# Emitting a fused linear-attention and SwiGLU kernel from group 2 on by a list scheduler, with Strassen pairs spread over six groups

## The chip, the cores and the metric

The kernel runs on one core of a Trainium2 chip. The metric is device time in microseconds (us), as the median over several executions; the profiled execution has a span of its own, about 2 us shorter. A run's ratio is the mean time of its fast runs over the mean of the fast runs of the kernel before, taken on the same chip in the same rounds, so it is not quite the ratio of the two medians that are quoted.

The engines are PE (TensorE, matmuls; PEld is its weight load), DVE (VectorE), ACT (ScalarE), POOL (GpSimd) and SP (SyncE, which issues DMAs here).

## The reference, cut to what matters

```python
# q, k, v: (8 batches, 8 heads, 576 positions, 64); phi(x) = elu(x) + 1
kv  = einsum('bhsd,bhde->...', phi(k), v);  z = sum_s phi(k)
x   = (phi(q) @ kv) / (phi(q) . z + 1e-6)          # 4608 tokens x 512
h   = silu(x @ w_gate) * (x @ w_val)               # "first layer", 512 -> 1536
out = h @ w_out                                    # "second layer", 1536 -> 512
```

The 4608 tokens are cut into nine groups of 512. While PE works on the two layers of group g, the other engines prepare batch g+1 ("the chain": z broadcast, denominators, scaling of q, transposes by DMA) and batch g+2 (the features phi of k and q, then kv).

## The kernel before

The kernel is hand-scheduled: the order in which the program emits instructions is the order in which each engine runs its own. The lists of closures below fix that order. In groups 7 and 8, ten of the twelve feature blocks (128 features each) of the first layer are done as five Strassen-Winograd pairs: seven products of 256 columns instead of eight, for additions on VectorE and copies on ScalarE.

```python
    def load(src, dst, b):                       # two buffers for k16, q16, v16 (and kp, qp, vm)
        nc.gpsimd.dma_start(out=dst[b % 2][:, :, :], in_=heads(src, b))

    def plus_1(src, dst, b, lp):                 # phi: max(x, 0) + 1, then min with exp(x)
        nc.vector.tensor_scalar(out=dst[b % 2][...], in0=src[b % 2][...], scalar1=0.0, scalar2=1.0,
                                op0=ALU.max, op1=ALU.add)

    def tr(b, c):                                # chain, third c: DMA transpose of the scaled q
        nc.sync.dma_start_transpose(out=qT[b % 2][...], in_=qp[b % 2][...])

    def joint(b):                                # kv of batch b ("J"), then the diagonals of z
        for lp in range(2): mm1(b, lp)
        for lp in range(2): zdiag(b, lp)         # VectorE, PSUM -> zd
        r_copies(b)                              # ScalarE
    ...
    for g in range(1, NG):                       # cut
        for fb in range(FB if g in TS else 0, FB):
            l1(g, fb)                            # 8 matmuls of 512 columns, silu, product
            for f in sl[fb]: f()                 # zb (z broadcast, a matmul that reads zd) after fb 1 or 2,
                                                 # thirds of the chain spread over the blocks, h sums
        for (i, step) in enumerate(l2_steps(g)): # second layer as Strassen products 10 11 20 21 60 ...
            ...
            if i == 12: mm2(b1, ...)             # "M": x of the next group
            for f in pre[i]: f()                 # phi of batch g+2
            if i == 12 and b2 < B: joint(b2)     # "J" right after "M"
```

Of the kernel before, what the change touches and what calls it, by code (L numbers as in the profile page):

```python
# [17 lines left out]
def kernel(  # L18
# [52 lines left out]
    xT = [two([P, U * C], FP16, f"xT{i}") for i in range(4)]  # L71
# [12 lines left out]
    id16 = sb.tile([P, P], FP16, name="id16")  # L84
    idx = sb.tile([P, P], mybir.dt.int32, name="idx")
# [7 lines left out]

    def load(src, dst, b):
        nc.gpsimd.dma_start(out=dst[b % 2][:, :, :], in_=heads(src, b))  # L95
# [22 lines left out]
    def exp_(src, e, b, lp):  # L118
        s = slice(2 * lp, 2 * lp + 2)
        nc.scalar.activation(out=e[:, s, :], in_=src[b % 2][:, s, :], func=AF.Exp, bias=0.0, scale=1.0)  # L120

    def plus_1(src, dst, b, lp):
        nc.vector.tensor_scalar(
            out=dst[b % 2][:, :, P * lp:P * lp + P].rearrange("p j (s d) -> p s j d", d=D),
            in0=src[b % 2][:, 2 * lp:2 * lp + 2, :].rearrange("p s (j d) -> p s j d", d=D), scalar1=0.0, scalar2=1.0,
            op0=ALU.max, op1=ALU.add)

    def least(e, dst, b, lp):
        d = dst[b % 2][:, :, P * lp:P * lp + P].rearrange("p j (s d) -> p s j d", d=D)
        nc.vector.tensor_tensor(out=d, in0=d, in1=e.rearrange("p s (j d) -> p s j d", d=D), op=ALU.min)  # L130
# [18 lines left out]
    def vcast(b, lp):  # L149
        s = slice(2 * lp, 2 * lp + 2)  # L150
        nc.scalar.activation(out=vm[b % 2][:, :, s, 0:D].rearrange("p j l d -> p l j d"),  # L151
                             in_=v16[b % 2][:, s, :].rearrange("p l (j d) -> p l j d", d=D),
                             func=AF.Copy, bias=0.0, scale=1.0)
# [4 lines left out]
    def terms_k(b, lp):  # L158

        return (kp[1], kp[0]) if b == 0 else (kp[b % 2],)  # L160

    def mm1(b, lp):
        if lp == 0:
            kvb[b] = ((pV[2], pX[0]), (pX[2], pV[2]), (pX[0], pX[1]), (pV[0], pG[0]), (pX[2], pV[2]))[min(b, 4)]
        for j in range(J):
            for (t, term_) in enumerate(terms_k(b, lp)):
                for hh in range(2):
# [7 lines left out]
                    for e in range(2):  # L175
# [4 lines left out]
                            rhs=v16[b][rows, 2 * lp + e, D * j:D * j + D] if b < 2 else vm[b % 2][rows, j, 2 * lp + e, :],  # L180
                            start=(j == 0), stop=(j == J - 1))

    def zdiag(b, lp):
        for hh in range(2):
            nc.vector.tensor_scalar(out=zd[:, 2 * hh + lp, :], in0=id16[:, :],
                                    scalar1=kvb[b][hh][:, 256 * lp + D:256 * lp + D + 1],
                                    scalar2=1.0 / SC, op0=ALU.mult, op1=ALU.mult)

    def r_copies(b):
        W = D  # L190
        for hh in range(2):
            nc.scalar.activation(out=R[b % 2][:, hh:4:2, 0:W],
                                 in_=kvb[b][hh][:, :].rearrange("p (i c) -> p i c", i=2)[:, :, 0:W], func=AF.Copy,
                                 bias=0.0, scale=1.0)
# [16 lines left out]
    def zb_copy(b):  # L211
        for hh in range(2):
            rows = slice(C * hh, C * hh + C)
            nc.scalar.activation(out=zbc[rows, :], in_=zps[b][rows, 256 * hh:256 * hh + 256], func=AF.Copy,
                                 bias=0.0, scale=1.0)
# [5 lines left out]
    def s3_prod(b, c):  # L221
        j0, j1 = js_of(c)
        nc.vector.tensor_tensor(out=prod[:, 0:j1 - j0, :], in0=qp[b % 2][:, j0:j1, :],
                                in1=zbc[:, :].unsqueeze(1).to_broadcast([P, j1 - j0, HL * D]), op=ALU.mult)
# [13 lines left out]
    def s3_scale(b, c):  # L238
        j0, j1 = js_of(c)
        qv = qp[b % 2][:, j0:j1, :].rearrange("p j (l d) -> p (j l) d", d=D)  # L240
# [4 lines left out]
    def tr(b, c):  # L245
        j0, j1 = js_of(c)
        nc.sync.dma_start_transpose(out=qT[b % 2][:, j0:j1, :, :].rearrange("p j l t -> p (j l) t"),
                                    in_=qp[b % 2][:, j0:j1, :].rearrange("p j c -> p (j c)"))
# [5 lines left out]
    def corners(ps, lhs, b, j0, j1, lps=(0, 1)):  # L254

        for lp in lps:
            for hh in range(2):
                for e in range(2):
                    rows = slice(D * e, D * e + D)
                    nc.tensor.matmul(out=ps[2 * lp + e][C * hh:C * hh + C, :], lhsT=lhs(2 * lp + hh, e),  # L260
                                     rhs=qT[b % 2][rows, j0:j1, lp, C * hh:C * hh + C], start=True, stop=True)

    def mm2(g, ps, engs):
        us = units(g)
        c00 = 2 * C if g == 2 else 0
        for b in sorted(set(u[0] for u in us)):
            js = [j for (bb, j) in us if bb == b]
            c0 = C * us.index((b, js[0]))
            if b > 1:
                corners([x[:, c0:c0 + C * len(js)] for x in ps], kv(b), b, js[0], js[-1] + 1)  # L270
        for i in range(4):
            dst = xT[i][g % 2][:, c00:]
            if engs[i] == "A":
                nc.scalar.activation(out=dst, in_=ps[i][:, c00:], func=AF.Copy, bias=0.0, scale=1.0 / SC)
            else:
                nc.vector.tensor_scalar(out=dst, in0=ps[i][:, c00:], scalar1=1.0 / SC, scalar2=None, op0=ALU.mult)  # L276
# [25 lines left out]
    TS = (NG - 2, NG - 1)  # L302
    HN = U * C // 2
    sbanks = ((pG[0], pV[0]), (pG[1], pV[1]), (pX[2], pV[2]))

    def flat(t):
        return t[:, :, :].rearrange("p a b -> p (a b)")

    wr = rr[:, :, :].rearrange("p a b -> p (a b)").bitcast(FP16)
    wl_all = ((wr[:, 0:10 * P], wr[:, 10 * P:20 * P]), (wl2[:, 0, :], wl2[:, 1, :]), (flat(k16[0]), flat(q16[0])),  # L310
              (flat(v16[0]), flat(kp[0])))

    def wl(m, c, f0, f1):
        return wl_all[m][c][:, P * f0:P * f1]

    def wl_sum(m, c, f0, f1):
        (g1, g2, v1, v2) = [w[:, i, P * f0:P * f1] for (w, i) in ((wg, c), (wg, 2 + c), (wv, c), (wv, 2 + c))]
        (a, b, op) = ((v1, v2, ALU.add), (wl(0, c, f0, f1), g1, ALU.subtract), (g1, v1, ALU.subtract),
                      (g2, wl(1, c, f0, f1), ALU.subtract))[m]
        nc.vector.tensor_tensor(out=wl(m, c, f0, f1), in0=a, in1=b, op=op)  # L320

    def x_blk(g, kh, th, c):
        return xT[2 * kh + c][g % 2][:, HN * th:HN * th + HN]

    def x_sum(g, m, c):
        (a, b) = ((x_blk(g, 0, 1, c), x_blk(g, 0, 0, c)), (x_blk(g, 1, 1, c), xs[:, 0, c, :]),
                  (x_blk(g, 1, 1, c), x_blk(g, 0, 1, c)), (x_blk(g, 1, 0, c), xs[:, 1, c, :]))[m]
        nc.vector.tensor_tensor(out=xs[:, m, c, :], in0=a, in1=b, op=ALU.subtract)

    def sp_prd(g, p, n):  # L330
        dst = sbanks[p % 3][1 if n in (2, 3, 5) else 0]
        for e in range(2):
            for c in range(2):
                fs = slice(P * (2 * p + e), P * (2 * p + e) + P)
                lhs = {1: wg[:, c, fs], 2: wg[:, 2 + c, fs], 4: wv[:, 2 + c, fs]}
                lhs = lhs[n] if n in lhs else wl({3: 3, 5: 0, 6: 1, 7: 2}[n], c, 2 * p + e, 2 * p + e + 1)
                rhs = {1: x_blk(g, 0, 0, c), 2: x_blk(g, 1, 0, c), 3: x_blk(g, 1, 1, c), 4: xs[:, 3, c, :],
                       5: xs[:, 0, c, :], 6: xs[:, 1, c, :], 7: xs[:, 2, c, :]}[n]
                nc.tensor.matmul(out=dst[:, HN * e:HN * e + HN], lhsT=lhs, rhs=rhs,  # L339
                                 start=(n in (1, 2, 5) and e == 0 and c == 0), stop=(c == 1), skip_group_check=True)  # L340
# [4 lines left out]
    def f32(t, n):  # L345
        return flat(t).bitcast(FP32)[:, 0:n]

    def sp_bufs(p):
        i = p % 2
        s12 = f32((k16, v16)[i][1], 4 * HN).rearrange("p (i e t) -> p i e t", i=2, e=2)  # L350
        s5 = f32(q16[1], 4 * HN)[:, 2 * HN * i:2 * HN * i + 2 * HN].rearrange("p (e t) -> p e t", e=2)
        gg = f32((kp[1], ek)[i], 4 * HN).rearrange("p (h e t) -> p h e t", h=2, e=2)
        sl = vm[i][:, :, :, :].rearrange("p j l d -> p (j l d)")[:, 0:4 * HN].rearrange("p (h e t) -> p h e t", h=2, e=2)
        v22 = flat(prod)[:, 2 * HN * i:2 * HN * i + 2 * HN].rearrange("p (e t) -> p e t", e=2)
        return (s12[:, 0, :, :], s12[:, 1, :, :], s5), gg, sl, v22

    def sp_keep(p, i, from_z, scale=1.0):
        nc.scalar.activation(out=sp_bufs(p)[0][i], in_=halves(sbanks[p % 3][from_z]), func=AF.Copy, bias=0.0, scale=scale)

    def sp_gadd(p, th):  # L360
        (s, gg, _, _) = sp_bufs(p)
        nc.vector.tensor_tensor(out=gg[:, th, :, :], in0=halves(sbanks[p % 3][1]), in1=s[th], op=ALU.add)

    def sp_silu(p, th):
        (_, gg, sl, _) = sp_bufs(p)
        nc.scalar.activation(out=sl[:, th, :, :], in_=gg[:, th, :, :], func=AF.Silu, bias=0.0, scale=1.0)  # L366

    def sp_v22(p):
        (s, _, _, v22) = sp_bufs(p)
        nc.vector.scalar_tensor_tensor(out=v22, in0=halves(sbanks[p % 3][0]), scalar=SC, in1=s[2], op0=ALU.mult, op1=ALU.add)  # L370

    def sp_h21(g, p):
        nc.vector.scalar_tensor_tensor(out=hT[g % 2][:, 2 * p:2 * p + 2, 0:HN], in0=halves(sbanks[p % 3][0]), scalar=SC,
# [624 lines left out]
```

## Time and profile before

The time before was 305.57 us (three runs, 305.49 to 305.88). First, the page of the profile of the kernel before: its span, the busy time of each engine with its share and number of instructions, and the shares of the chain that ended last.

```profile
span 303.4 us, 6676 instructions
...
PE 295.6 (97%) x2596; PEld 181.0 (60%) x2596; DVE 247.6 (82%) x526; ACT 193.1 (64%) x313; POOL 49.2 (16%) x61
...
PE 89%; issue 4%; DMA 2%; ACT 1%; DVE 1%; POOL 0%; POOLq 0%; DVEq 0%; ACTq 0%
```

PE is the limit. Its busy time alone would not say so (matmuls overlap: the page gives one of 512 columns 379 ns, and the next one starts after 216), but the starts of the matmuls do. I took the distance of every two successive starts in the trace: 216 ns after a matmul of 512 columns and 109 ns after one of 256 is work; about 90 ns on top of that, at a change between matmuls on the full array and on quarters of it, is a mode change; what is above that is a wait. These sums are from 85 us (start of group 2) to the last matmul:

| kernel before | work | mode changes | waits |
|---|---|---|---|
| us | 211.4 | 1.0 | 0.9 |

Finally the DMA transposes of group 4 in the kernel before, from the view of one tile, qT, in a window from 150 to 182 us (first and last start, then the time from issue to landing):

```profile
L247 SPq DMA_TRANSPOSE qT<-qp x3: 1211/1211/1212, 158.6 to 168.9; - x3
...
DMA to landing us min/median/max: 2.7/2.7/2.7
```

They are issued between 158.6 and 168.9 us and land after 2.7 us. The kernel has two buffers for qp, so nothing of the next batch waits for them.

Of stretches (the view of windows), the busy time of VectorE was 28.4 of 31.5 us in each of groups 3 to 5.

### The profile page before, as it was taken

To read this page: it belongs to the slowest core of one execution; us is meant where nothing else is said; L and a number is where in the kernel's file an instruction comes from. 1 tells how busy PE (TensorE), PEld (TensorE's weight loads), DVE (VectorE), ACT (ScalarE), POOL (GpSimd) and SP (SyncE) were. 2 spreads that over 40 slices of the span, in tenths; PEclk is the share of its full clock that TensorE was granted. 3 is DMA by queue.
4 is the path that set the end of the run, shared out by engine and by line. 5 is a ranking of instruction groups with operands and counts; after the bars stand their busy time and mean duration, and the time that the engine had idled before them with its cause. 6 is when DMAs were issued, how large, how long until landed. Compare 5 with 4: busy or idle time off the path is not lost.

```text
span 303.4 us, 6676 instructions
## 1 busy us (share of the span) xinstructions
PE 295.6 (97%) x2596; PEld 181.0 (60%) x2596; DVE 247.6 (82%) x526; ACT 193.1 (64%) x313; POOL 49.2 (16%) x61
## 2 busy tenths in 40 slices
PE   7899999999999999999999999999999999999993
PEld 5644454444544485448644774477446888878882
DVE  4754649888859998998799889987999878968991
ACT  4864978858563698358846685568633478548931
POOL 8664256310010001000100000000000004001300
PEclk9999999999999999999999999999999999999998
DMA  8999999999979229911892132123312050033014
GB/s 214 193 196 201 206 208 220 199 212 191 133 147 154 51 31 201 190 34 29 173 197 56 28 81 62 34 46 71 71 26 54 22 119 0 2 74 67 2 37 104
DMA packets 41472, 32.88 MB, mean 108 GB/s; under 512 B 16400, under 2 KB 36816, under 8 KB 41440
## 3 DMA queue, kind: packets, MB, share of 16 engines
q0 software_dynamic: 20176, 18.35, 39.1%
q1 hardware_dynamic: 21104, 13.97, 20.1%
q8 instruction: 20, 0.33, 0.5%
q10 hardware_dynamic: 160, 0.13, 0.2%
q14 instruction: 12, 0.10, 0.1%
HBM read 37.75 MB, written 9.44 MB: 156 GB/s over the span
## 4 chain that ended last, share of the span: by engine, by line
PE 89%; issue 4%; DMA 2%; ACT 1%; DVE 1%; POOL 0%; POOLq 0%; DVEq 0%; ACTq 0%
PE pV L287 23%; PE pG L287 21%; PE pX L502 14%; PE pV L502 4%; PE pV L339 4%; PE pG L339 4%; PE pG L446 4%; PE pV L446 4%; PE pX L287 3%; DMA q<-in_q_dram 2%; PE pV L260 1%; PE pX L260 1%; PE pX L339 1%; PE pX L177 1%; PE pV L407 1%
## 5 line engine op out<-in xcount | busy, mean ns | idle before, releaser
L287 PE MATMUL pV<-xT,wv 128*128 128x512 f16 x324 | 83.5, 379 | 0.0
L287 PE MATMUL pG<-xT,wg 128*128 128x512 f16 x296 | 76.4, 379 | 0.0
L292 ACT ACTIVATE sil<-pG 128x512 f16<-128x512 f32 x74 | 43.5, 597 | 47.1 <-PE pG L287 32.2
L293 DVE SCALAR_TENSOR_TENSOR hT<-pV,sil 128x512 f16<-128x512 f32 x81 | 55.0, 686 | 15.0 <-PE pV L287 7.6
L287 PEld LDWEIGHTS <-wv 128*128 128x128 f16 x336 | 32.9, 98 | 39.7
L287 PEld LDWEIGHTS <-wg 128*128 128x128 f16 x336 | 32.3, 98 | 39.1 <-DVE xT L276 0.8
L502 PEld LDWEIGHTS <-hs 128*128 128x128 f16 x336 | 32.5, 98 | 4.7 <-DVE hs L476 0.4
L379 POOL TENSOR_TENSOR hT<-prod,vm 128x512 f16<-128x512 f16 x6 | 6.9, 1152 | 127.5 <-ACT vm L366 127.5
L502 PEld LDWEIGHTS <-hT 128*128 128x128 f16 x252 | 24.3, 98 | 4.1
L502 PE MATMUL pX<-ws,hs 128*128 128x256 f16 x210 | 25.7, 273 | 0.0
L507 ACT ACTIVATE part<-pX 128x256 f32<-128x256 f32 x35 | 12.8, 380 | 13.2 <-PE pX L502 13.2
L476 DVE TENSOR_TENSOR hs<-hT 128x512 f16<-128x512 f16 (+2 forms) x42 | 17.4, 418 | 0.2
L241 DVE TENSOR_TENSOR qp<-qp,rden 128x768 f16<-128x768 f16 x18 | 17.1, 948 | 0.0
L228 DVE TENSOR_REDUCE den<-prod 128x12 f32<-128x768 f16 x18 | 16.9, 942 | 0.0
L120 ACT ACTIVATE ek<-k 128x1152 f16<-128x1152 f16 x14 | 16.1, 1160 | 1.2 <-DMA k<-in_k_dram 1.1
L95 POOL DMA_DIRECT2D k<-in_k_dram x7 | 5.2, 745 | 64.1 <-ACT part L507 44.0
L502 PE MATMUL pX<-wo,hT 128*128 128x256 f16 x126 | 15.2, 273 | 0.0
L130 DVE TENSOR_TENSOR kp<-kp,ek 128x1152 f16<-128x1152 f16 x14 | 10.6, 758 | 5.4 <-ACT ek L120 5.0
L446 PEld LDWEIGHTS <-hT 128*128 128x128 f16 x96 | 8.7, 98 | 10.3 <-issue 0.8
L151 ACT ACTIVATE vm<-v 128x1152 f16<-128x1152 f16 x12 | 14.1, 1173 | 0.0
L120 ACT ACTIVATE eq<-q 128x1152 f16<-128x1152 f16 x12 | 13.3, 1169 | 0.0
L512 DVE SCALAR_TENSOR_TENSOR osb<-pX,part 128x256 f32<-128x256 f32 x28 | 11.0, 418 | 2.1 <-PE pX L502 1.9
(186 smaller groups left out, 513.7 us busy)
## 6 DMA issues: line engine op xcount, KB each, us to landing
out_dram<-osb SPq DMA_DIRECT2D x64, 128.0 KB, 3.0
k<-in_k_dram POOLq DMA_DIRECT2D x7, 576.0 KB, 8.8
q<-in_q_dram POOLq DMA_DIRECT2D x7, 576.0 KB, 11.4
v<-in_v_dram POOLq DMA_DIRECT2D x7, 576.0 KB, 13.5
wg<-in_moe_w_gate_dram POOLq DMA_DIRECT2D x5, 256.0 KB, 9.0
wv<-in_moe_w_val_dram POOLq DMA_DIRECT2D x5, 256.0 KB, 9.2
wo<-in_moe_w_out_dram POOLq DMA_DIRECT2D x2, 512.0 KB, 15.1
out_dram<-osb SPq DMA_DIRECT2D x13, 64.0 KB, 2.0
```

The source lines that it names most:

```text
L120: nc.scalar.activation(out=e[:, s, :], in_=src[b % 2][:, s, :], func=AF.Exp, bias=0.0, scale=1.0)
L151: nc.scalar.activation(out=vm[b % 2][:, :, s, 0:D].rearrange("p j l d -> p l j d"), in_=v16[b % 2][:, s, :].rearrange("p l (j d) -> p l j ...
L228: nc.vector.tensor_reduce(out=den[:, HL * j0:HL * j1], in_=prod[:, 0:j1 - j0, :].rearrange("p j (l d) -> p (j l) d", d=D), axis=AX.X, op=A ...
L241: nc.vector.tensor_tensor(out=qv, in0=qv, in1=rden[:, HL * j0:HL * j1].unsqueeze(2).to_broadcast([P, HL * (j1 - j0), D]), op=ALU.mult)
L287: nc.tensor.matmul(out=ps[:, :], lhsT=src[:, i, P * fb:P * fb + P], rhs=xT[i][g % 2][:, :], start=(i == 0), stop=(i == 3))
L292: nc.scalar.activation(out=s[:, :], in_=pg[:, :], func=AF.Silu, bias=0.0, scale=1.0)
L293: nc.vector.scalar_tensor_tensor(out=hT[g % 2][:, fb, :], in0=pv[:, :], scalar=SC, in1=s[:, :], op0=ALU.mult, op1=ALU.mult)
L339: nc.tensor.matmul(out=dst[:, HN * e:HN * e + HN], lhsT=lhs, rhs=rhs, start=(n in (1, 2, 5) and e == 0 and c == 0), stop=(c == 1), skip_gr ...
L446: nc.tensor.matmul(out=pso[(g, t)][:, :], lhsT=hT[g % 2][:, fb, P * t:P * t + P], rhs=wo[:, fb, :], start=(fb == 0), stop=(fb == FB - 1))
L476: (eng or nc.vector).tensor_tensor(out=o, in0=a, in1=b, op=op)
L502: nc.tensor.matmul(out=(z if n in (2, 3, 5) else x)[:, 0:HD], lhsT=left(f), rhs=right(f), start=(f == 0 and n in (1, 2, 5)), stop=(f == HF ...
L507: nc.scalar.activation(out=part[:, 2 * i + tt, :], in_=(x if from_x else z)[:, 0:HD], func=AF.Copy, bias=0.0, scale=1.0 / SC)
```

## The change

The change has three intents. From group 2 on, a list scheduler orders the instructions instead of the hand-made lists: every operation is declared with its engine, a modelled duration, and the names it reads and writes; a simulation with modelled durations and lags then picks the order for ScalarE and VectorE (PE, GpSimd and SyncE keep the program's order). Strassen pairs go from ten to 24: two in each of groups 3 to 5, six in each of 6 to 8. And product 1 of a pair is copied by ScalarE into another PSUM bank (PSUM is the memory that matmuls write to, here the tiles pG, pV and pX), on which product 2 accumulates, which takes one addition per pair off VectorE. To hold the extra weight sums, the even buffers of k16, q16, v16, kp and vm are given up from batch 3 on: one function, `ix`, decides the buffer. The diff has over 900 lines; this is its core:

```diff
+    def ix(b):
+        return b % 2 if b < 3 else 1
+
     def load(src, dst, b):
-        nc.gpsimd.dma_start(out=dst[b % 2][:, :, :], in_=heads(src, b))
+        nc.gpsimd.dma_start(out=dst[ix(b)][:, :, :], in_=heads(src, b))
 ...
     def plus_1(src, dst, b, lp):
-            out=dst[b % 2][:, :, P * lp:P * lp + P]...,
-            in0=src[b % 2][:, 2 * lp:2 * lp + 2, :]...,
+            out=dst[ix(b)][:, :, P * lp:P * lp + P]...,
+            in0=src[ix(b)][:, 2 * lp:2 * lp + 2, :]...,
 ...
     def tr(b, c):
-                                    in_=qp[b % 2][:, j0:j1, :]...)
+                                    in_=qp[ix(b)][:, j0:j1, :]...)
 ...
+    wl_all = [sum((thirds(t) for t in ts), []) for ts in (
+        (k16[0][:, :, :], q16[0][:, :, :], v16[0][:, :, :]), (kp[0][:, :, :], wl2[:, :, :], vm[0][:, :, :, :]))]
 ...
+    LAG = dict(PE=0.2, ACT=0.18, DVE=0.18, POOL=0.3, SP=2.7, LD=9.0)
+    ops = []
+    def op(eng, t, f, r=(), w=()):
+        ops.append((eng, t, f, tuple(r), tuple(w)))
+    def arrange():            # cut: dependencies from the names, then at each step the ready
+        ...                   # operation that can start first; within 0.2 us, the most urgent
+    NP = {2: 0, 3: 2, 4: 2, 5: 2, 6: 6, 7: 6, 8: 6}
 ...
+        if n == 1:
+            op("ACT", 0.52, lambda: keep_1(bx, halves(by)), [nm(bx)], [nm(by)])      # the seed
 ...
+    ZB = {g: 2 for g in range(NG)}                    # z broadcast after 2 chunks (0.86 us) of a group
+    XE = {g: "AVAA" for g in range(NG)}               # engines of the four x copies
+    ORDER = {g: "10 11 20 21 60 61 50 51 70 71 30 M 31 40 J 41" for g in (2, 3, 4)}
+    ORDER[5] = "10 11 20 21 60 61 50 51 70 71 M 30 31 | 40 41 J"
 ...
+    program()
+    for i in arrange():
+        ops[i][2]()
```

## The prediction

> **What bounds it now.** TensorE. In the page it is busy 97% and PE work is 89% of the chain that ended last. In the timeline from group 2 on, matmul starts are 216 ns (512 columns) or 109 ns (256 columns) apart almost without a break: start-to-start distances beyond those two sum to about 2.0 us between 85 and 298 us, mostly the ~93 ns at each change between full and quarter-array matmuls (M and J steps). So a better order has almost no PE wait to remove. VectorE is second: 28.5 of 31.5 us busy per group in groups 3 to 5 (windows).
>
> **Removed from PE.** Two plain feature blocks are 16 x 216 = 3.456 us; one Strassen pair is 28 x 109 = 3.056 us; a pair saves 0.40 us. Pairs go from 10 (five in groups 7 and 8) to 24 (two in 3-5, six in 6-8): 14 more, so 5.6 us: 0.8 in each of groups 3-5, 2.4 in group 6, 0.4 in 7 and 8.
>
> **Added to PE.** M and J are no longer adjacent (groups 2-5) and M is split in 6-7: two more array mode changes each, 6 x 0.19 = 1.1 us. Waits of 0.07-0.10 us at group boundaries may go (-0.3). Floor: 305.6 - 5.6 + 1.1 - 0.3 = about 300.8 us.
>
> **Other engines.** Durations in the profile overlap: back to back the 686 ns PSUM product on VectorE recurs every 601 ns, reduce 860, scale 866, prod 411, least 676, 128x512 fp16 sum 335, ScalarE activation 493. (The Trainium skill, "Perfetto Trace Analysis", Per-instruction lifecycle, says the window holds the write acknowledgement; this trace agrees, 686 against 601.) With these a pair costs VectorE 3 x 601 + 335 = 2.1 us against 1.2 for the plain blocks (the PSUM seed has already removed one 0.6 us add). ScalarE: 5 x 0.5 against 2 x 0.5. Estimated VectorE issue time per group after: group 2 31.9 us (eight weight sums of 0.47 added), 3 and 4 30.4, 5 29.9, group 6 about 28, against PE 31.6, 30.9, 30.9, 28.4. Before: about 27.3 of 31.5. So VectorE has no slack in groups 2-6, and its in-order queue will at times hold what PE needs. I estimate 1-2 us of new PE waits there, and about 0.3 us in each of groups 6-8 after the sixth pair, where no plain blocks are left to cover its latency.
>
> The seed costs no PE time: ScalarE copies product 1 into another bank and product 2 adds there. The Trainium skill, "PSUM — Partial Sum Buffer", The four PSUM rules, says ScalarE writes leave the accumulate bits alone; no run here shows it yet.
>
> **Prediction.** 300.8 + about 1.6 = 302.4 us; 8 in 10 between 300.7 and 304.5. Faster by over 2%: 0.05; within 2%: 0.92; slower: 0.03.
>
> **What would show it.** Windows: group 6 shorter by about 2 us, 7-8 hardly, groups 3-5 by only 0.2-0.6 us each, group 2 longer by 0-0.5. VectorE busy over 95% in groups 2-5. Waits: new PE (weight load) waits on VectorE hT, hs, xs or on xT. Up to group 2 and after the last matmul: unchanged. If groups 3-5 each gain 0.6 us, VectorE was not limiting.
>
> **What would make it wrong.** The static order's modelled lags (loads 9 us, transposes 2.7 us) may differ from the chip: ScalarE could block on a value cast for some us. Or the order hides VectorE and the floor is reached.

## More of the kernel before

The batches of runs were taken on several chips, and the kernel before took 305.4 to 305.9 us in them; a small difference between runs of different batches is therefore read from the ratios.

The timeline of VectorE in the kernel before, at the end of group 4 (start us, duration us, engine, line, operation, output<-inputs, count, and in brackets the idle time before and what ended it):

```profile
178.00 1.29 DVE L276 TENSOR_SCALAR xT<-pG 128x512 f16<-128x512 f32 x2 [0.75 <-PE pG L260]
179.21 0.25 DVE L185 TENSOR_SCALAR zd<-id,pX 128x128 f16<-128x128 f16 x1
...
179.70 0.25 DVE L185 TENSOR_SCALAR zd<-id,pV 128x128 f16<-128x128 f16 x1
179.87 0.45 DVE L123 TENSOR_SCALAR qp<-q 128x1152 f16<-128x1152 f16 x1
```

The four diagonals of z (`zd`) come first and the next batch's query features (`qp<-q`) behind them. The timeline of PE at the same place:

```profile
181.95 1.03 PE L287 MATMUL pV<-xT,wv 128*128 128x512 f16 x4
182.81 0.38 PE L208 MATMUL pX<-zd,ones 128*128 128x512 f16 x1
183.03 1.03 PE L287 MATMUL pG<-xT,wg 128*128 128x512 f16 x4
```

The z broadcast (`pX<-zd,ones`) starts 3.46 us into group 5 (179.35 us) and waits for nothing.

## The result, and the profile after

The change took 310.69 us (four runs, 309.70 to 311.52) against 305.60 us for the kernel before in the same rounds: ratio 1.0164, 95% interval 1.013 to 1.0198. It is 1.6% slower where I had predicted 1% faster, and outside the range that I gave.

The page after, the same lines:

```profile
span 309.4 us, 7044 instructions
...
PE 294.9 (95%) x2764; PEld 197.7 (64%) x2764; DVE 262.6 (85%) x561; ACT 217.1 (70%) x361; POOL 42.4 (14%) x55
...
PE 47%; issue 38%; DVE 6%; DMA 5%; ACT 1%; POOL 1%; POOLq 0%; DVEq 0%
```

| from 85 us to the last matmul, us | work | mode changes | waits |
|---|---|---|---|
| before | 211.4 | 1.0 | 0.9 |
| after | 206.6 | 1.9 | 10.2 |

The share of "issue" in the chain, 4% before and 38% now, is time for which the view finds no releaser; it is a sign that PE no longer runs through, and the sums of the distances say how much. So the saving is there: 4.8 us of work by these sums, and up to 5.7 us in the variants below, for the 5.6 that I had predicted. The mode changes cost 0.9 us (predicted 1.1). But PE waits 9.3 us longer. By groups the waits are 0.7 (group 2), 0.3, 2.1, 4.7, 0.9, 0.9 and 0.6 us (group 8): the two largest lie at the starts of groups 4 and 5. Apart from the half clock described below, no other single wait of PE is longer than 0.7 us. The view of waits of the change (who waited for whom: us in total, times, longest) names both:

```profile
PE pX L214 <- DVE zd L193: 3.6, 2, 2.3
DVE qp L128 <- DMA qT<-qp: 3.4, 2, 2.0
```

The timeline of VectorE in the change, at the end of group 4 and the start of group 5:

```profile
180.91 0.42 DVE L336 TENSOR_TENSOR xs<-xt 128x512 f16<-128x512 f16 x1
183.29 0.46 DVE L128 TENSOR_SCALAR qp<-q 128x1152 f16<-128x1152 f16 x1 [1.97 <-DMA qT<-qp]
183.67 0.26 DVE L193 TENSOR_SCALAR zd<-id,pX 128x128 f16<-128x128 f16 x1
...
185.04 0.26 DVE L193 TENSOR_SCALAR zd<-id,pV 128x128 f16<-128x128 f16 x1 [0.34 <-ACT R L198]
```

VectorE stands still for 1.97 us. The query features of batch 6 (`qp<-q`) wait for the third DMA transpose of batch 5, which still reads the same buffer. The diagonals of z stand behind them in the queue, though their own input has been there since the J matmuls, about 181 us. The timeline of PE at the same place:

```profile
182.00 1.03 PE L934 MATMUL pG<-xt,wg 128*128 128x512 f16 x4
185.35 0.59 PE L214 MATMUL pX<-zd,ones 128*128 128x512 f16 x1 [2.32 <-DVE zd L193]
185.73 1.06 PE L934 MATMUL pV<-xt,wv 128*128 128x512 f16 x2
```

The z broadcast waits 2.32 us for the diagonals, and the matmuls behind it wait as long. In the kernel before, VectorE had the diagonals first, and the broadcast stood 2.6 us later in the group. The qT tile of the change, from 164 to 186 us:

```profile
L251 SPq DMA_TRANSPOSE qT<-qp x2: 1310/1334/1359, 176.7 to 178.2; - x2
...
  DVE qp L128: 2.0, 1
...
DMA to landing us min/median/max: 5.0/5.4/5.9
```

The third transpose of group 4 is issued 29.3 us after the start of the group (178.2 less 148.9 us), before it was 21.1 us (168.9 less 147.8), because VectorE comes to the third part of the chain late; the last two transposes are issued 1.5 us apart, and they take 5.9 and 5.0 us to land, not 2.7. The k load of batch 7 is in flight: it was issued at 175.39 us and landed after 6.37 us. The Trainium skill, "Trainium Kernel Development and Optimization", Key Constraints, says that DMAs issued from SyncE, ScalarE and GpSimd run on the same 16 DMA engines and interleave. This trace agrees: from group 2 on, the transposes that overlap a load take 3.1 to 5.9 us, the others 2.7 to 2.8, with one of 3.6. A short overlap need not show: in the kernel before, two transposes that overlapped the end of a v load for 1.6 to 1.7 us still took 2.7 us.

That VectorE cannot pass a waiting instruction is what the Trainium skill says too ("PSUM — Partial Sum Buffer", Engine vs sequencer instructions: the queues of ScalarE, VectorE and GpSimd are strict first in, first out), and the trace agrees with 1.97 us in which ready work stood behind.

Windows of the change at this wait (length; busy us and count of PE, PEld, VectorE, ScalarE and GpSimd; then the granted clock of PE, DMA share and GB/s):

```profile
183.00:184.00 1.00, 0.03 (x1) 0.00 (x0) 0.63 (x2) 0.04 (x1) 0.00 (x0) 1.00 1.09 391
184.00:184.90 0.90, 0.00 (x0) 0.00 (x0) 0.43 (x2) 0.41 (x2) 0.00 (x0) 1.00 0.93 209
184.90:185.70 0.80, 0.35 (x1) 0.10 (x1) 0.66 (x3) 0.80 (x3) 0.00 (x0) 0.63 0.17 59
185.70:188.30 2.60, 2.60 (x10) 1.22 (x9) 2.40 (x5) 1.39 (x4) 0.43 (x1) 0.50 0.46 102
```

The wait has an echo: PE's clock is halved from 185.11 to 188.52 us (3.41 us by the trace's clock record), which costs about 1.5 us more by the distances of the starts. The Trainium skill, "TensorE: Matmul & The Clock Gate", What's actually happening, describes a half-rate state set by a free-running window of 3413 ns, and the length agrees. It also fits the spread of the four runs: 309.70 and 310.25 us came with a mean granted clock of 0.997, 311.12 and 311.52 us with 0.992 and 0.994. That the latter two had one more window at half clock is my reading; only the profiled one (311.12 us) has a trace.

### The profile page after: what moved, and what is told of

It is laid out like the page before. It is cut to its first block, busy times and chain, and to the rows that moved or that the text cites. A ratio compares the mean times of both kernels' runs of the same rounds, so it can differ in the third digit from the quotient of the medians.

```text
span 309.4 us, 7044 instructions
## 1 busy us (share of the span) xinstructions
PE 294.9 (95%) x2764; PEld 197.7 (64%) x2764; DVE 262.6 (85%) x561; ACT 217.1 (70%) x361; POOL 42.4 (14%) x55
## 4 chain that ended last, share of the span: by engine, by line
PE 47%; issue 38%; DVE 6%; DMA 5%; ACT 1%; POOL 1%; POOLq 0%; DVEq 0%
PE pV L934 7%; PE pG L934 6%; PE pV L293 6%; PE pX L440 5%; PE pG L293 4%; PE pX L293 4%; PE pG L379 4%; PE pV L379 3%; DMA qT<-qp 3%; PE pX L347 2%; DMA q<-in_q_dram 2%; PE pX L264 1%; PE pV L440 1%; DVE zd L193 1%; DVE qp L135 1%
## 5 line engine op out<-in xcount | busy, mean ns | idle before, releaser
L934 PE MATMUL pV<-xt,wv 128*128 128x512 f16 x144 | 39.8, 386 | 0.0
L934 PE MATMUL pG<-xt,wg 128*128 128x512 f16 x144 | 38.4, 379 | 0.0
L364 ACT ACTIVATE sil<-pG 128x512 f16<-128x512 f32 x36 | 21.4, 593 | 22.6 <-PE pG L934 21.4
L440 PEld LDWEIGHTS <-hs 128*128 128x128 f16 x336 | 32.4, 98 | 5.2 <-issue 1.0
L440 PEld LDWEIGHTS <-hT 128*128 128x128 f16 x252 | 24.1, 98 | 4.7 <-DVE hs L409 0.4
L370 DVE SCALAR_TENSOR_TENSOR hT<-pV,sil 128x512 f16<-128x512 f32 x36 | 24.6, 682 | 0.8 <-PE pV L934 0.7
L934 PEld LDWEIGHTS <-wv 128*128 128x128 f16 x144 | 14.2, 99 | 15.1 <-issue 2.9
L347 PEld LDWEIGHTS <-wg 128*128 128x128 f16 x192 | 18.9, 99 | 5.6 <-issue 1.0
L293 PE MATMUL pV<-xt,wv 128*128 128x512 f16 x84 | 21.9, 379 | 0.0
L299 DVE SCALAR_TENSOR_TENSOR hT<-pV,sil 128x512 f16<-128x512 f32 x21 | 14.2, 689 | 9.0 <-ACT sil L298 4.9
L934 PEld LDWEIGHTS <-wg 128*128 128x128 f16 x144 | 14.1, 98 | 11.9
L364 ACT ACTIVATE ek<-eq 128x512 f16<-128x512 f32 x24 | 15.0, 624 | 7.2 <-DVE eq L963 7.1
L347 PE MATMUL pV<-xt,wg 128*128 128x256 f16 x120 | 17.0, 273 | 0.0
L440 PE MATMUL pX<-wo,hT 128*128 128x256 f16 x126 | 16.9, 273 | 0.0
L449 ACT ACTIVATE part<-pX 128x256 f32<-128x256 f32 x35 | 12.4, 389 | 6.1 <-PE pX L440 6.0
L293 PEld LDWEIGHTS <-wv 128*128 128x128 f16 x96 | 9.4, 98 | 11.3
```

Of the source, the lines that this page charges most:

```text
L293: nc.tensor.matmul(out=ps[:, :], lhsT=src[:, i, P * fb:P * fb + P], rhs=xT[i][g % 2][:, :], start=(i == 0), stop=(i == 3))
L299: nc.vector.scalar_tensor_tensor(out=hT[g % 2][:, fb, :], in0=pv[:, :], scalar=SC, in1=s[:, :], op0=ALU.mult, op1=ALU.mult)
L347: nc.tensor.matmul(out=dst[:, HN * e:HN * e + HN], lhsT=lhs, rhs=rhs, start=(n in (1, 5) and e == 0 and c == 0), stop=(c == 1), skip_group ...
L364: nc.scalar.activation(out=dst, in_=src, func=AF.Silu, bias=0.0, scale=1.0)
L370: nc.vector.scalar_tensor_tensor(out=hT[g % 2][:, fb, :], in0=pv[:, :], scalar=SC, in1=s[:, :], op0=ALU.mult, op1=ALU.mult)
L440: nc.tensor.matmul(out=(z if n in (2, 3, 5) else x)[:, 0:HD], lhsT=left(f), rhs=right(f), start=(i == 0 and fs[0] == 0 and (n in (1, 5) or ...
```

## The experiments

Eighteen kernels were run in five batches, all correct. The theories:

- Theory 1: the qp buffer shared by successive batches makes VectorE wait for a transpose, and all that stands behind waits with it.
- Theory 2: VectorE is full, as the prediction had it; the waits are lack of throughput.
- Theory 3: the z broadcast merely stands too early in PE's order.
- Theory 4: the scheduler's modelled lags (transposes 2.7 us, loads 9.0 us) are too short, so the static order puts instructions ahead of others that turn out to be ready sooner.
- Theory 5: any reshuffle gives another time; what a constant does is luck.
- Theory 6: the transposes land late because they overlap the k load.

In the texts, "the third run" is e3_np0 and "the fourth run" e4_splag. All results in one table. "Waits" are PE's, with matmuls at half clock, as defined above; the ratio is to the kernel before in the same rounds.

| kernel | time, us | ratio | work | mode changes | waits |
|---|---|---|---|---|---|
| the change | 310.69 | 1.0164 | 206.6 | 1.9 | 10.2 |
| e1_qp2 | 307.43 | 1.0057 | 206.1 | 1.9 | 6.8 |
| e2_zb8 | 308.43 | 1.009 | 205.9 | 1.8 | 8.2 |
| e3_np0 | 311.19 | 1.0182 | 208.6 | 1.9 | 7.8 |
| e4_splag | 305.12 | 0.9983 | 206.6 | 1.9 | 4.2 |
| e5_lags | 307.02 | 1.0042 | 206.3 | 1.8 | 6.5 |
| e6_np0_lags | 305.87 | 1.0003 | 208.6 | 1.9 | 2.7 |
| e7_qp2_lags | 305.51 | 0.9994 | 205.7 | 1.9 | 5.3 |
| e8_splag4 | 305.88 | 1.0012 | 206.2 | 1.9 | 5.5 |
| e9_relief | 310.38 | 1.017 | 206.0 | 1.9 | 10.0 |
| e10_qp2_relief | 308.10 | 1.0089 | 205.7 | 1.9 | 7.9 |
| e11_qp2_rel_mj | 308.04 | 1.0085 | 206.6 | 1.4 | 8.0 |
| e12_relief_only | 319.30 | 1.0453 | 206.4 | 1.8 | 18.1 |
| e13_qvk | 307.81 | 1.0073 | 206.5 | 1.9 | 6.6 |
| e14_qp2_xact | 304.39 | 0.9959 | 206.0 | 1.9 | 4.3 |
| e15_np1 | 305.46 | 0.9993 | 207.4 | 1.4 | 4.5 |
| e16_np0_mj | 305.95 | 1.0011 | 208.3 | 1.4 | 3.7 |
| e17_m1 | 304.66 | 0.9964 | 206.1 | 1.6 | 4.4 |
| e18_m1_mj | 305.37 | 0.9986 | 206.6 | 1.1 | 5.4 |

### e1_qp2: two buffers for the query features, same order

```diff
+    def iq(dst, b):
+        return b % 2 if dst is qp else ix(b)
-            out=dst[ix(b)][:, :, P * lp:P * lp + P]...      # plus_1 and least
+            out=dst[iq(dst, b)][:, :, P * lp:P * lp + P]...
-    ... qp[ix(b)] ...                                        # product, scale, transpose of the chain
+    ... qp[b % 2] ...
```

> The only edit: the query features of batches 3 on get two buffers again (batch parity), as in the kernel before. The order on every engine is unchanged, checked instruction by instruction. Theory 1 (shared buffer): the longest PE waits (1.4 us in group 4, 2.5 us plus 1.4 us of half clock in group 5) come from VectorE standing still 1.4 and 2.0 us at the head of its queue, where the next batch's query features wait for the third transpose of the batch before, out of the same buffer. Then those VectorE waits vanish and the time falls by 4 to 5.5 us, to 305 to 307. Rival, theory 2 (VectorE is simply full): the wait at the z broadcast matmul stays or moves, and the time stays above 309.

It took 307.43 us (306.90 to 307.77). The even qp buffer had been free all along: the weight sums do not use it. The order of instructions on every engine is the same, and so is VectorE's work, so only the wait is taken away. The timeline of VectorE in e1_qp2 at the place shown above:

```profile
179.67 0.42 DVE L339 TENSOR_TENSOR xs<-xt 128x512 f16<-128x512 f16 x1
180.00 0.46 DVE L131 TENSOR_SCALAR qp<-q 128x1152 f16<-128x1152 f16 x1
180.37 0.26 DVE L196 TENSOR_SCALAR zd<-id,pX 128x128 f16<-128x128 f16 x1
```

VectorE no longer stands still, the wait at the z broadcast falls to 0.4 us in group 5 and to nothing over 0.1 us in group 4, and the clock is not halved there. About 3.3 us of the 5.1 us loss are gone. Theory 1 holds for that part; it falls 0.4 us short of the range that I wrote down, for 6.8 us of waits remain, at more places than before (the largest 1.1 us).

### e2_zb8: the z broadcast later on PE

```diff
-    ZB = {g: 2 for g in range(NG)}
+    ZB = {g: 8 for g in range(NG)}
```

> The z broadcast matmul stands after 8 chunks of the first layer instead of 2 (about 5 us later on PE); the list scheduler then orders VectorE and ScalarE anew. Theory 3 (the wait is only placed too early on PE): PE no longer waits there, 305 to 306.5. Theory 1: the VectorE waits of 1.4 and 2.0 us stay, PE is shielded from most of them: 306 to 308. Theory 2: PE waits turn up at other matmuls, time 309 to 312.

It took 308.43 us, just above what theory 1 expected and below theory 2. No wait at the broadcast is left, but 8.2 us of waits are, spread over the pairs and the starts of products, and VectorE still stands 1.8 us at the transpose. Placing was a part, not the cause. ScalarE and VectorE were reordered with it, so this run is a weaker test than the first.

### e3_np0 and e6_np0_lags: no pairs in groups 3 to 5, without and with longer lags

```diff
-    NP = {2: 0, 3: 2, 4: 2, 5: 2, 6: 6, 7: 6, 8: 6}
+    NP = {2: 0, 3: 0, 4: 0, 5: 0, 6: 6, 7: 6, 8: 6}                               # both
-    LAG = dict(PE=0.2, ACT=0.18, DVE=0.18, POOL=0.3, SP=2.7, LD=9.0)
+    LAG = dict(PE=0.2, ACT=0.18, DVE=0.18, POOL=0.3, SP=5.0, LD=13.0)             # e6_np0_lags only
```

> No Strassen pairs in groups 3 to 5, six in 6 to 8 as in the change: 6 pairs less, so PE has 2.4 us more and VectorE about 2.2 us less in each of the three groups. Theories 1 and 2 both: VectorE finishes the chain earlier, the third transposes are issued earlier, the waits in groups 4 and 5 shrink below 0.5 us; net 306 to 307.5. If the pairs were not the cause of the lateness but the scheduler's order were, the waits stay and the time rises to about 313.

It took 311.19 us, against 306 to 307.5 expected: a miss, and the one that taught most. VectorE has about 2 us less to do in each of the three groups (two pairs at 2.1 against 1.2 us, by the estimate of the prediction), yet PE waits 7.8 us. The view of waits of e3_np0 shows where:

```profile
ACT vm L156 <- DMA v<-in_v_dram: 7.0, 4, 2.9
```

With time to spare, the scheduler puts the cast of v on ScalarE as soon as its model has the load landed. The trace has v landing 10.9 to 12.4 us after issue; the model has 9.75. ScalarE stands 7.0 us in all, the activations behind it wait, and PE waits for their products. VectorE also stands 1.5 us at a transpose. That is theory 4 at a second place.

> No pairs in groups 3 to 5 as in the third run, with transposes at 5.0 and loads at 13.0 us in the model. In the third run ScalarE stood 7.0 us on value loads and VectorE 1.5 us on a transpose. Theory 4: both waits vanish, PE waits fall from 7.8 us to below 3.5: 306 to 308 (PE work is 2.4 us more than with the pairs). If VectorE work rules, it should even beat the run with pairs. If it stays near 311, theory 4 falls.

With both lags longer, the same kernel took 305.87 us; the 7.0 us and the 1.5 us are gone and PE's waits fall from 7.8 to 2.7 us. Two constants of the model are worth 5.3 us here, with the same PE order. Without the pairs in groups 3 to 5 and with the model's old lags the kernel is as slow as the change. A loss of that size thus needs no pairs there; but it sits mostly at another wait (ScalarE at the casts), so this does not show that the waits of the change itself would have come without them.

### e4_splag, e8_splag4, e5_lags: the lags alone

```diff
-    LAG = dict(PE=0.2, ACT=0.18, DVE=0.18, POOL=0.3, SP=2.7, LD=9.0)
+    LAG = dict(PE=0.2, ACT=0.18, DVE=0.18, POOL=0.3, SP=5.0, LD=9.0)     # e4_splag
+    LAG = dict(PE=0.2, ACT=0.18, DVE=0.18, POOL=0.3, SP=4.0, LD=9.0)     # e8_splag4
+    LAG = dict(PE=0.2, ACT=0.18, DVE=0.18, POOL=0.3, SP=5.0, LD=13.0)    # e5_lags
```

> One constant of the scheduler's model: a transpose is taken to land 5.0 us after issue instead of 2.7 (measured here 2.8 to 5.9). Same PE order. Theory 1: the scheduler then puts the diagonals of z ahead of the query features that wait, or issues the transposes sooner, and the PE waits in groups 4 and 5 shrink: 306 to 309. Theory 2: 309.5 to 312, as before.

> Transpose lag 4.0 us, loads 9.0 as in the change: between the change (2.7) and the fourth run (5.0). Theory 4: the measured landings of the third transposes are 3.9 and 5.0 us, so 4.0 helps in part, 305 to 308, monotonic in the lag. Theory 5: no order, may be worse than 310.

> The change with both lags of the scheduler's model set to what the traces show: transposes 5.0 us (was 2.7) and loads 13.0 us (was 9.0; value loads took 8 to 12.4). PE order unchanged. Theory 4 (the static order is wrong because the modelled lags are too short, and in-order queues then stand still): at least as good as with the transpose lag alone, 304 to 305.3. Rival, theory 5 (any reshuffle gives another time, the lag was luck): anywhere from 304 to 311.

They took 305.12, 305.88 and 307.02 us. One constant, the transpose lag, takes the change from 310.69 to 305.12 us. The timeline of VectorE in e4_splag at the end of group 4:

```profile
179.74 0.42 DVE L336 TENSOR_TENSOR xs<-xt 128x512 f16<-128x512 f16 x1
180.08 0.25 DVE L193 TENSOR_SCALAR zd<-id,pX 128x128 f16<-128x128 f16 x1
...
184.19 0.82 DVE L128 TENSOR_SCALAR kp<-k 128x1152 f16<-128x1152 f16 x2
184.93 0.46 DVE L128 TENSOR_SCALAR qp<-q 128x1152 f16<-128x1152 f16 x1
```

The diagonals come first now, and the query features start 4.9 us after them; the transpose, issued at 179.85 us, has landed by then (after 3.28 us). The times fall with the lag: 310.7, 305.9 and 305.1 us for 2.7, 4.0 and 5.0. But with the longer load lag as well, the kernel is 1.9 us slower than without it: a miss. The 6.5 us of waits in e5_lags have a new largest one of 1.1 us before kv of batch 7. So theory 4 explains the large waits: none of the three kernels has a wait of VectorE at a transpose left. Theory 5 is right about the rest: the order alone moved the time by 1.9 us between e4_splag and e5_lags. What about the order makes that difference was not found, and how much of the 5.6 us that e4_splag returns is such luck is not known.

### e7_qp2_lags: lags and buffer together

```diff
+    (as e1_qp2, and the scheduler's names for qp by batch parity, as e5_lags for the lags)
+    def rqp(b, c=(0, 1, 2), lps=(0, 1)):
+        return [f"qp{b % 2}.{lp}.{k}" for lp in lps for k in c]
```

> Both lags as before, and two buffers for the query features, of which the scheduler now knows (names by batch parity). Theory 1 with 4: one more constraint gone, 303 to 305. If VectorE is simply full, no gain over the run with lags alone: within 0.5 us of it.

It took 305.51 us, 1.5 us less than e5_lags, but half a microsecond above the range. The second buffer is worth less once the model's lags are longer; e5_lags has no wait of VectorE at a transpose left for it to remove. The 1.5 us are within what a new order can do by itself.

### e12_relief_only, e9_relief, e10_qp2_relief, e11_qp2_rel_mj: VectorE relieved

```diff
-    XE = {g: "AVAA" for g in range(NG)}
+    XE = {g: "AAAA" for g in range(NG)}
-                pair_prd(g, p, PSEQ[0][k], (pX[1], pX[0])[p % 2], pX[2], pV[1], "DVE")
+                pair_prd(g, p, PSEQ[0][k], (pX[1], pX[0])[p % 2], pX[2], pV[1], "POOL")
     # e12_relief_only: nothing else;  e9_relief: SP=5.0
     # e10_qp2_relief: as e7_qp2_lags; e11_qp2_rel_mj: as e10, and ORDER "... 30 31 40 M J 41" in groups 2 to 4
```

> The change with VectorE relieved of about 1.3 us per group and nothing else: all four x copies on ScalarE (one of 0.6 us moves), and the product that makes the last quarter of hT in groups 3 to 5 on GpSimd (two of 0.335 us move). Modelled lags as in the change (2.7 and 9). Theory 2 (VectorE full is the cause): the lateness of the third transposes goes, 304 to 306. Theory 4 (the lags): VectorE still stands at the query features behind a transpose that lands later than modelled, 307 to 310.

> The same relief with the transpose lag at 5.0 us, to be compared with the run that had this lag alone (305.12 us, 4.1 us of PE waits from 85 us on). If full VectorE holds up PE in the rest of the waits: PE waits fall to about 2.5 us, 303 to 304.2. If what is left has another cause (bank hand-overs, ends of the first layer): within 0.5 us of 305.1.

> Two query buffers known to the scheduler, lags 5.0 and 13.0, and the same relief; against the run without relief (305.51 us). VectorE-full theory: 303 to 304.3. Otherwise 305 to 306.

> As the last one, and M and J adjacent again in groups 2 to 4 (order 30 31 40 M J 41, as in the kernel before). Saves two array mode changes of 0.09 us in each of three groups and gives the bank that J writes more time to be read: 0.6 to 1.5 us less than without, 302 to 303.5. If the x copies after the later M come too late for the next group, no gain.

They took 319.30, 310.38, 308.10 and 308.04 us. The first three are each slower than their counterparts with the fuller VectorE (the change 310.69, e4_splag 305.12, e7_qp2_lags 305.51), and the fourth gained nothing on the third. None of the theories had expected that. The view of waits of e12_relief_only:

```profile
DVE qp L128 <- DMA qT<-qp: 8.8, 3, 4.0
ACT ek L364 <- DVE eq L963: 8.4, 9, 2.1
PE pX L182 <- DVE osb L454: 6.8, 2, 3.6
```

A VectorE with less to do comes to the query features earlier and stands longer: 8.8 us instead of 3.4. And it comes to the third scale earlier, so the third transposes are issued at 142.69 and 180.64 us, within 0.9 us after the k loads (141.88 and 180.40 us), and land after 6.34 and 6.75 us. Behind the waiting features stand the outputs (`osb`) that free a PSUM bank for J, and PE waits 3.4 and 3.8 us there; the clock of PE halves after each (152.8 to 156.2 and 190.3 to 193.7 us). The same happens with the lag at 5.0 us, since 6.7 is more than 5.0. The timeline of VectorE in e9_relief:

```profile
183.25 0.46 DVE L128 TENSOR_SCALAR qp<-q 128x1152 f16<-128x1152 f16 x1 [1.93 <-DMA qT<-qp]
```

If lack of VectorE time were the cause, as the prediction had it, e12_relief_only should have helped. It was 8.6 us slower. These runs are not clean, though: the scheduler ordered ScalarE and VectorE anew, and GpSimd takes 1.15 to 1.42 us for the product that VectorE makes in 0.42, and the h sums need its result (the view of waits has VectorE waiting for GpSimd's product only once, for 0.3 us in e12_relief_only). With two buffers there is no such wait at a transpose, and e10_qp2_relief is still 2.6 us slower than e7_qp2_lags, with PE waits of about 0.5 us before products that read h sums. That loss may be GpSimd's slower product; no run shows it alone.

### e13_qvk: the k load last

```diff
-            for (f, x) in ((ld_k, "k16"), (ld_q, "q16"), (ld_v, "v16")):
+            for (f, x) in ((ld_q, "q16"), (ld_v, "v16"), (ld_k, "k16")):
```

> The change with the three loads of a batch issued in the order q, v, k instead of k, q, v in the second layer, and nothing else: PE, ScalarE and SyncE orders unchanged, VectorE moves 5 instructions. All three loads now start only when the query buffer is free, so no load overlaps the third transpose. Theory 6 (the transpose lands late because it shares the DMA engines with the k load): third transposes of groups 3 and 4 land in 2.7 to 3.0 us instead of 3.9 and 5.0, VectorE's waits of 1.4 and 2.0 us fall to below 0.5, time 305.5 to 308. If the transposes land late anyway, 309.5 to 311.5.

It took 307.81 us. Besides the loads, five instructions of VectorE move. The q load must wait until the q features have been made, so now no load starts before them. The qT tile of e13_qvk, from 164 to 186 us:

```profile
L251 SPq DMA_TRANSPOSE qT<-qp x2: 1210/1211/1212, 175.6 to 177.1; - x2
...
DMA to landing us min/median/max: 2.7/2.7/2.7
```

And the timeline of VectorE at the same place:

```profile
180.21 0.45 DVE L128 TENSOR_SCALAR qp<-q 128x1152 f16<-128x1152 f16 x1
180.58 0.25 DVE L193 TENSOR_SCALAR zd<-id,pX 128x128 f16<-128x128 f16 x1
```

The two transposes are issued 1.5 us apart as in the change, but land in 2.7 us. The query features still stand ahead of the diagonals, but no longer wait, and the time falls by 2.9 us, almost as much as with the second buffer (3.3 us), by quite another edit. Theory 6 holds for these transposes: the lag of 2.7 us in the model was right for them alone, and wrong beside the k load.

### e14_qp2_xact, e15_np1, e16_np0_mj: VectorE relieved without GpSimd, and fewer pairs

```diff
     # all three: as e7_qp2_lags, and
-    XE = {g: "AVAA" for g in range(NG)}
+    XE = {g: "AAAA" for g in range(NG)}
     # e15_np1: one pair in groups 3 to 5, ORDER "... 30 31 40 M J 41" in groups 2 to 4; e16_np0_mj: no pair there
```

> Two query buffers, lags 5.0 and 13.0 (305.51 us) and all x copies on ScalarE, no GpSimd: VectorE 0.6 us lighter per group. If full VectorE rules the rest: 304 to 305. If not: 305 to 306.

> As e14, one pair instead of two in groups 3 to 5, and M next to J in groups 2 to 4. PE work 1.2 us more and 0.55 us less for the mode changes, VectorE 0.9 us less per group. If full VectorE costs PE waits with two pairs (5.2 us against 2.7 without): 303.8 to 305.

> As e15 with no pair in groups 3 to 5: PE work 2.4 us more than with two, 0.55 us less for the mode changes, waits 2 to 2.7 us: 304.5 to 305.6, a little under the kernel before.

They took 304.39, 305.46 and 305.95 us: the first within what theory 2 expected of it, the other two 0.5 and 0.35 us above their ranges. e14_qp2_xact is faster than both kernels (ratio 0.9959, interval 0.9941 to 0.9977). One copy of 0.6 us per group moved from VectorE to ScalarE took off 1.1 us against e7_qp2_lags, and the waits fell from 5.3 to 4.3 us. That would fit a full VectorE costing about 1 us once the standing still is gone, the size that the prediction gave to the whole. It is not shown: the scheduler ordered ScalarE and VectorE anew here too, and a new order alone moved the time by 1.9 us above. The windows of e14_qp2_xact still show VectorE busy 31.42 of 32.0 us from 148 to 180 us. Fewer pairs do not help: against e14_qp2_xact, one pair spares nothing in waits (4.5 against 4.3 us) and no pair 0.6 us, and they add 1.4 and 2.3 us of work.

### e17_m1, e18_m1_mj: fewer mode changes

```diff
     # e17_m1: as e14_qp2_xact, M of groups 6 and 7 in one piece; e18_m1_mj: also M next to J in groups 2 to 4
-        ORDER[g] = "10c 11c 20c 21c M0 10d 11d 20d 21d M1 60 61 50 51 70 71 30 | 31 40 41"
+        ORDER[g] = "10c 11c 20c 21c 10d 11d M 20d 21d 60 61 50 51 70 71 30 | 31 40 41"
```

> As e14 (304.39 us), with M of groups 6 and 7 in one piece after the first products instead of two halves: two array mode pairs less, 2 x 0.19 = 0.37 us. Expected 303.6 to 304.6; if above 305.4 the e14 result is sensitive to order and partly luck.

> As e17, and M next to J in groups 2 to 4 as in the kernel before: another 3 x 0.19 = 0.55 us of mode changes less, 303 to 304.3. In the relief run with GpSimd this gave nothing (308.1 to 308.0), so a later x copy may give it back: then equal to e17.

With five rounds they took 304.66 and 305.37 us, 0.06 and 1.1 us above what was expected (ratios 0.9964, interval 0.9952 to 0.9977, and 0.9986, interval 0.9974 to 0.9999). The mode changes fell as counted, from 1.9 to 1.6 and 1.1 us. The waits hardly changed in the first (4.4 against 4.3 us) and rose by 1.1 us in the second. e17_m1 confirms e14_qp2_xact under a small change of order; neither beats it. That a change of tiling mode drains the engine is stated by the Trainium skill, "TensorEngine Tiling (Array Packing)", Key Properties; the traces show a break of about 0.09 us each way.

## Why the prediction was wrong

- **What bounds the kernel before, and what the pairs save: right.** PE had 0.9 us of waits from group 2 on, and 14 more pairs took 4.8 to 5.7 us of work away in the variants with all pairs (predicted 5.6). The extra mode changes cost 0.9 us (predicted 1.1).
- **The PSUM seed: right.** Results are correct, so product 2 did add to what ScalarE had written, as the Trainium skill, "PSUM — Partial Sum Buffer", The four PSUM rules, has it for elements whose accumulate bit a previous matmul has set.
- **The step that failed: "I estimate 1-2 us of new PE waits there".** I had derived the waits in groups 2 to 6 from throughput: 31.9 and 30.4 us of VectorE work against 31.6 and 30.9 of PE. Measured were 8.7 us of waits in groups 2 to 6 (0.7, 0.3, 2.1, 4.7, 0.9). The largest of them come from order and a buffer: VectorE stood 1.4 and 2.0 us at query features that shared a buffer with a transpose still under way, ready diagonals stood behind them, PE stood behind the diagonals, and in the profiled run the clock then halved. Taking away the sharing (e1_qp2) or the late landing (e13_qvk) returns 3.3 and 2.9 us; giving the scheduler a longer transpose lag returns 5.6 us (e4_splag; 3.7 with the load lag longer too, e5_lags). Taking VectorE work away did not cure it (e12_relief_only, though that run is not clean). Not all is explained: of the 9.3 us of new waits e1_qp2 takes away 3.4 and e4_splag 6.0, and the 3.3 us that e4_splag keeps above the kernel before, no run accounts for. What is left is a little above the sum that I had estimated (1-2 us, and 0.3 us in each of groups 6 to 8).
- **I read the diff for costs and not for lifetimes.** The function `ix` was in it, and its effect on qp is a new write-after-read dependency on a DMA; in the kernel before, qp had two buffers and the third transpose came 8 us earlier in the group.
- **What I named under "What would make it wrong" pointed at the cause,** with the wrong engine in front. The modelled lags were off, but in the change itself VectorE stood at a transpose (3.4 us), and ScalarE at value casts only 1.0 us. The case that I had described, ScalarE at the casts, appeared in e3_np0 with 7.0 us. I gave this a place in the text and no weight in the range.
- **VectorE full: nearly right as a fact, its cost not shown.** I had it over 95% busy in groups 2 to 5. It was busy 31.6 of 32.4, 29.7 of 31.4, 31.6 of 33.1 and 30.3 of 33.4 us in groups 2 to 5. What that costs by itself is not shown; e14_qp2_xact against e7_qp2_lags, 1.1 us, is a hint, no larger than what a new order can do.
- **The signs I listed:** group 2 was to be longer by 0 to 0.5 us, and was by 1.0. Groups 3 to 5 were to be shorter by 0.2 to 0.6 us each: group 3 was by 0.2, groups 4 and 5 were longer by 1.6 and 1.9. Group 6 was to be shorter by about 2, and was by 1.1 although it took over the last products of group 5. The largest new waits of PE were at zd, which I had not listed.
- **The waits after the sixth pair in groups 6 to 8** were 0.9, 0.9 and 0.6 us by group, where I had put 0.3 each; they also stand in e14_qp2_xact, in part.

What stays open: why e5_lags is 1.9 us slower than e4_splag with a load lag nearer to the measured one, and in general the 1 to 2 us by which equally sound orders differ; what the 3.3 us of new waits in e4_splag are; and how much a full VectorE costs. And whether GpSimd's slower product alone explains e10_qp2_relief.

## What to carry to other kernels

When a buffer loses its double, list who still reads it when the next writer comes: a wait for a DMA in an in-order queue costs all that stands behind it, and may cost a clock window on top. A scheduler with fixed lags should be given the landing time of a DMA beside the loads that will run at that moment, not its time alone, and the traces of the first run should be used to set them before anything else is tuned. And a full engine is not yet a limit: take work away from it in one run before you believe it.

## What the Trainium skill lacked or had wrong

- "TensorE: Matmul & The Clock Gate", What's actually happening, has the half clock after at least one idle window of about 3.4 us. Here the clock halved at 185.11 us after PE had stood only from 183.03 us on (2.1 us); the half-rate stretch itself was 3.41 us long, the length of the page's window. Waits of 1.4 us (group 4) and 1.9 us (e9_relief) brought no half clock. All clock changes inside a trace lie on a grid of 3.41 us. Cut along it, and counted by the starts of the matmuls, the windows just before a half clock held 2.2 us (the change), 2.4 and 3.1 us (e12_relief_only) of standing PE, and no other window from 20 us on in the twenty traces held more than 1.9 us; so in these traces a window with PE idle for two thirds of it was enough, and one with 1.9 us was not.
- No page that I looked up has the landing time of a DMA transpose from SBUF to SBUF of a size like this (128 partitions by 768 elements of 16 bits): from 85 us on in the twenty traces, 2.7 to 2.9 us for 138 of the 167 that overlap no load of 576 KB (the others up to 4.5), 2.7 to 6.8 us beside a k load alone, and up to 11.6 us beside q and v loads together (e11_qp2_rel_mj).
- "TensorEngine Tiling (Array Packing)", Key Properties, says that a mode change drains PE and gives no cost there: about 0.09 us each way, between full-array matmuls and matmuls on quarters of the array.
